# The W1 and W3 blocks of a streamed FFN in transfers of 256 rows instead of 512

## The chip, the cores and the metric

The kernel runs on one core of a Trainium2 chip, in one launch. The metric is the device time of that core in microseconds (us), the median of several executions. The profile comes from one execution, taken by the hardware profiler.

## The reference

The input is `x`, 2048 tokens of 576 features, in bfloat16. Four residual blocks follow each other: a recurrent attention layer, a gated FFN, and the same two once more with the same weights.

```python
x = x + _A_ref(_layernorm(x), mem0, Wq, Wk, Wv, Wo, seg_len=32)   # 64 segments, 8 memory rows carried along
x = x + _B_ref(_layernorm(x), w1, w3, w2)
x = x + _A_ref(_layernorm(x), mem0, Wq, Wk, Wv, Wo, seg_len=32)
x = x + _B_ref(_layernorm(x), w1, w3, w2)

def _B_ref(x, w1, w3, w2):                 # w1, w3: 576 x 4608; w2: 4608 x 576
    gate = jnp.einsum('bsd,df->bsf', x, w1)
    up   = jnp.einsum('bsd,df->bsf', x, w3)
    return jnp.einsum('bsf,fd->bsd', _silu(gate) * up, w2)
```

The attention layer takes 32 tokens at a time; each segment attends to itself and to 8 memory rows that the segment before has produced, so its 64 segments are a chain. It has 32 heads of 128.

## The kernel before

The two attention layers run interleaved: the second follows the first by eight segments, and each of the 72 steps handles one segment of each layer, where both are under way. All attention weights stay in SBUF. The FFN works on groups of 128 tokens (four segments). A job takes a group of the first layer and, where there is one, a group of the second together, 256 columns, and goes through 4608 hidden features in 18 blocks of 256, called pairs. Its weights are too large to stay, so every job streams them from HBM again.

For a pair, `load_w13` fills one of two slots of the tile `W13` (128 partitions x 9 chunks x 256 columns, bfloat16). Chunks 0 to 3 hold rows 0 to 511 of W1, chunks 4 to 7 those of W3, and chunk 8 holds the last 64 rows of both, W1 in partitions 0 to 63 and W3 in partitions 64 to 127. The text calls the first two *blocks* and the last two *tails*. `load_w2` fills one of two slots of `W2C`.

On TensorE the pair is two pieces of work that stand apart in the order. `ffn_up` without `tail` (letter `F` in the order) multiplies the eight chunks of the blocks; `ffn_up` with `tail` (letter `f`) multiplies the tails, in the mode in which TensorE works on two halves of 64 rows. Each run of matmuls begins with the weight load (LDWEIGHTS) that waits for its transfer. Tanh on ScalarE, two products on VectorE and `ffn_down` with W2 follow.

The order of TensorE's work is written out by hand as strings of letters (`FIRST`, `FOUR` eleven times, `LAST`). Everything else is ordered by `plan`, a list scheduler that runs when the kernel is built, with an estimated duration for each piece and with slots as resources; a `W13` load is one piece in it, whatever number of transfers it issues. The order so found is then fixed on every engine. All loads named above are issued by SyncE (SP in the profile), one after the other, from `dma` (line 600). An issue waits until TensorE has read the old content of the place, and the program gives SP's transfers eight semaphores in turn, so that an issue also waits until the transfer eight places before it has landed. The trace shows these as SP's waits for PE and for DMA.

The last job of all finds the attention weights no longer needed and loads its FFN weights into their place in larger transfers (`tail_load`).

Of the kernel before, what the change touches and what calls it, by code (L numbers as in the profile page):

```python
# [13 lines left out]
P = 128  # L14
# [553 lines left out]
class Emitter:  # L568
# [122 lines left out]
    def load_w13(self, pr, w13):  # L691
        def f(n):
            fa = pr * 2 * P
            W = self.T.W13[:, w13.i]
            for kind, wd in ((0, self.a.w1), (1, self.a.w3)):
                self.dma(W[:, 4 * kind:4 * kind + 4], wd[0:4 * P, fa:fa + 2 * P].rearrange("(c p) f -> p c f", p=P))
            for kind, wd in ((0, self.a.w1), (1, self.a.w3)):
                self.dma(W[kind * R64:(kind + 1) * R64, 8], wd[4 * P:D, fa:fa + 2 * P])
        return f
# [628 lines left out]
```

## Time and profile before

| | |
|---|---|
| median of 7 runs | 2695.61 us (2690.09 to 2698.95) |
| the profiled execution | 2695.15 us, span 2693.4 us |
| granted TensorE clock, mean | 0.994 |
| PE (matmul) busy | 2628.0 us, 98% of the span |
| DVE, ACT, POOL busy | 78%, 51%, 12% |
| `W13` loads | 306: 612 blocks of 256 KB, 612 tails of 32 KB |
| `W2C` loads | 306 of 288 KB |
| moved by DMA | 322.08 MB, mean 120 GB/s |

PE is TensorE's matmuls, PEld its weight loads, DVE is VectorE, ACT ScalarE, POOL GpSimd; SPq is SyncE's queue, which issues transfers. A row of a wait says who waited for whom, the sum in us, how often, and the longest. In a timeline the first column is the start in us, the second the time from the first instruction's start to the last one's end, and what stands in brackets is the idle time before and what ended it. Line 591 of the kernel records every matmul, line 594 every operation of ScalarE, line 597 every one of VectorE, and line 600 every transfer that SP issues, so groups are told apart by tiles. The tiles `W13` and `W` both show as `W`; a transfer `W<-in_B_w_dram` fills `W13`, but for 16 of the last job.

### The profile page before, as it was taken

To read this page: it belongs to the slowest core of one execution; us is meant where nothing else is said; L and a number is where in the kernel's file an instruction comes from. 1 tells how busy PE (TensorE), PEld (TensorE's weight loads), DVE (VectorE), ACT (ScalarE), POOL (GpSimd) and SP (SyncE) were. 2 spreads that over 40 slices of the span, in tenths; PEclk is the share of its full clock that TensorE was granted. 3 is DMA by queue.
4 is the path that set the end of the run, shared out by engine and by line. 5 is a ranking of instruction groups with operands and counts; after the bars stand their busy time and mean duration, and the time that the engine had idled before them with its cause. 6 is when DMAs were issued, how large, how long until landed. Compare 5 with 4: busy or idle time off the path is not lost.

```text
span 2693.4 us, 137075 instructions
## 1 busy us (share of the span) xinstructions
PE 2628.0 (98%) x60995; PEld 2285.4 (85%) x60995; DVE 2103.3 (78%) x5463; ACT 1362.8 (51%) x3938; POOL 332.4 (12%) x400
## 2 busy tenths in 40 slices
PE   5999999999999999999999999999999999999998
PEld 4788888888888888888888888888888888888886
DVE  5787886887878788787878878787877878787776
ACT  2655554544545454454545455454545545454542
POOL 1111110110101011010101101010111101011110
PEclk8999999999999999999999999999999999999999
DMA  9064524243442334344233434424243442434457
GB/s 317 5 185 128 149 84 129 78 128 109 117 126 80 111 88 128 108 117 126 80 113 86 128 108 117 127 80 118 83 125 108 117 129 67 118 89 135 128 168 246
DMA packets 478178, 322.08 MB, mean 120 GB/s; under 512 B 26024, under 2 KB 467760, under 8 KB 476944
## 3 DMA queue, kind: packets, MB, share of 16 engines
q1 hardware_dynamic: 474048, 305.43, 38.6%
q8 instruction: 477, 7.82, 1.2%
q0 software_dynamic: 3024, 6.93, 0.9%
q10 hardware_dynamic: 512, 0.94, 0.2%
q14 instruction: 117, 0.96, 0.1%
HBM read 308.49 MB, written 2.36 MB: 115 GB/s over the span
## 4 chain that ended last, share of the span: by engine, by line
PE 86%; DVE 5%; DMA 3%; ACT 3%; issue 1%; SPq 1%; POOL 0%; ACTq 0%; DVEq 0%
PE bank L591 86%; DMA W<-in_B_w_dram 2%; ACT V L594 2%; DVE STAT L597 1%; SPq L600 1%; DVE HTT L597 1%; DVE PB L597 1%; DVE SME L597 1%; DMA W<-in_A_Wk_dram 1%; DVE V L597 1%; DMA WO<-in_A_Wo_dram 0%; DMA XN<-in_A_x_dram 0%; ACT PTS L594 0%; ACT SME L594 0%; DVE PTS L597 0%
## 5 line engine op out<-in xcount | busy, mean ns | idle before, releaser
L591 PEld LDWEIGHTS <-W 128*128 128x128 bf16 (+2 forms) x32176 | 1266.7, 100 | 129.8 <-issue 60.4
L591 PE MATMUL bank<-HT,W 128*128 128x80 bf16 (+3 forms) x23040 | 810.6, 197 | 18.9 <-issue 7.7
L591 PE MATMUL bank<-XTB,W 128*64 128x256 bf16 (+5 forms) x9136 | 660.6, 263 | 6.8 <-DMA W<-in_B_w_dram 3.2
L594 ACT ACTIVATE QKT<-bank 128x64 bf16<-128x64 f32 (+2 forms) x1500 | 349.7, 311 | 351.1 <-PE bank L591 345.1
L1006 POOL MEMSET PB<- 128x1024 bf16 x288 | 274.1, 952 | 1832.4 <-PE bank L591 1539.7
L591 PE MATMUL bank<-OT,WO 128*128 128x80 bf16 (+3 forms) x11520 | 407.5, 198 | 3.4 <-ACT OT L594 1.3
L591 PEld LDWEIGHTS <-WO 128*128 128x128 bf16 (+1 forms) x11520 | 380.4, 102 | 20.8 <-issue 8.9
L594 ACT ACTIVATE V<-bank 64x512 bf16<-64x512 f32 (+1 forms) x606 | 343.1, 585 | 94.7 <-PE bank L591 86.0
L591 PE MATMUL bank<-WV,HT 128*32 128x512 bf16 (+5 forms) x3584 | 373.8, 382 | 1.6 <-DMA WV<-in_A_Wv_dram 1.0
L591 PE MATMUL bank<-W2C,HTT 128*64 128x288 bf16 (+1 forms) x3072 | 322.8, 286 | 1.5 <-issue 1.0
L597 DVE TENSOR_REDUCE STAT<-SME 104x8 f32<-104x320 f32 (+1 forms) x576 | 274.3, 476 | 10.7 <-ACT SME L594 5.3
L597 DVE TENSOR_TENSOR PB<-SME,STAT 40x128 bf16<-40x128 f32 (+4 forms) x912 | 274.9, 336 | 8.5 <-DVE STAT L597 0.5
L594 ACT ACTIVATE HTT<-bank 128x512 bf16<-128x512 f32 (+1 forms) x324 | 176.6, 553 | 206.6 <-PE bank L591 205.0
L597 DVE SCALAR_TENSOR_TENSOR XR<-bank,XR 128x288 f32<-128x288 f32 x576 | 245.9, 446 | 24.2 <-PE bank L591 20.0
L591 PEld LDWEIGHTS <-HT 128*32 128x32 bf16 (+5 forms) x3584 | 154.2, 98 | 125.4 <-issue 17.9
L597 DVE SCALAR_TENSOR_TENSOR HTT<-HTT,bank 128x512 bf16<-128x512 bf16 (+1 forms) x324 | 201.7, 623 | 74.5 <-ACT HTT L594 70.5
L591 PEld LDWEIGHTS <-HTT 128*64 128x64 bf16 (+1 forms) x3136 | 223.5, 105 | 35.3 <-issue 2.5
L594 ACT ACTIVATE OT<-bank 128x320 bf16<-128x320 f32 (+1 forms) x420 | 155.2, 403 | 148.9 <-PE bank L591 146.0
L597 DVE TENSOR_TENSOR HTT<-HTT,bank 128x512 bf16<-128x512 bf16 (+1 forms) x324 | 203.6, 628 | 27.8 <-DVE HTT L597 0.5
L594 ACT ACTIVATE SME<-SME 104x320 f32<-104x320 f32 (+1 forms) x288 | 135.2, 470 | 166.5 <-DVE SME L597 164.7
L597 DVE CAST QKT<-bank 128x128 bf16<-128x128 f32 (+4 forms) x548 | 147.7, 317 | 83.5 <-PE bank L591 81.3
L594 ACT ACTIVATE PTS<-bank 128x320 bf16<-128x320 f32 (+1 forms) x383 | 143.8, 403 | 133.2 <-PE bank L591 120.1
(61 smaller groups left out, 1831.7 us busy)
## 6 DMA issues: line engine op xcount, KB each, us to landing
W<-in_B_w_dram SPq DMA_DIRECT2D x612, 256.0 KB, 3.6
W2C<-in_B_w_dram SPq DMA_DIRECT2D x306, 288.0 KB, 3.3
W<-in_B_w_dram SPq DMA_DIRECT2D x612, 32.0 KB, 3.4
W<-in_B_w_dram SPq DMA_DIRECT2D x8, 1024.0 KB, 12.4
W<-in_A_Wq_dram SPq DMA_DIRECT2D x9, 512.0 KB, 9.2
WO<-in_A_Wo_dram SPq DMA_DIRECT2D x4, 1152.0 KB, 18.1
XR<-in_A_x_dram POOLq DMA_DIRECT2D x16, 288.0 KB, 3.6
WV<-in_B_w_dram SPq DMA_DIRECT2D x4, 1152.0 KB, 10.4
```

The lines of the kernel that those rows point to most:

```text
L591: self.ch("PE", self.nc.tensor.matmul(out, lhsT=lhsT, rhs=rhs, start=start, stop=stop, skip_group_check=True, **k))
L594: self.ch("ACT", self.nc.scalar.activation(*a, **k))
L597: self.ch("DVE", getattr(self.nc.vector, fn_)(*a, **k))
L600: self.ch("SP", self.nc.sync.dma_start(out=out, in_=in_))
L1006: return lambda n: self.ch("POOL", self.nc.gpsimd.memset(self.T.PB[:, pb.i], 0.0))
```

## The change

Each block of 512 rows is loaded in two transfers of 256 rows (two chunks each). The tails stay as they are, and still come after all blocks of the load. A load thus issues six transfers, four of 128 KB and two of 32 KB, instead of four, two of 256 KB and two of 32 KB.

```diff
             W = self.T.W13[:, w13.i]
             for kind, wd in ((0, self.a.w1), (1, self.a.w3)):
-                self.dma(W[:, 4 * kind:4 * kind + 4], wd[0:4 * P, fa:fa + 2 * P].rearrange("(c p) f -> p c f", p=P))
+                for c in (0, 2):
+                    self.dma(W[:, 4 * kind + c:4 * kind + c + 2], wd[c * P:(c + 2) * P, fa:fa + 2 * P].rearrange("(c p) f -> p c f", p=P))
             for kind, wd in ((0, self.a.w1), (1, self.a.w3)):
                 self.dma(W[kind * R64:(kind + 1) * R64, 8], wd[4 * P:D, fa:fa + 2 * P])
```

The order of instructions on PE, DVE, ACT and POOL is the same in both built programs. On SP the 612 blocks become 1224, at the same places. In the built programs SP's transfers rise from 1592 to 2204, and PE's waits on transfers from 1564 to 2178: the first weight load of every half of a block now waits for its own transfer.

## The prediction

> **What bounds the kernel now.** First the page's busy times and the chain that ended last.
>
> ```profile
> PE 2628.0 (98%) x60995; PEld 2285.4 (85%) x60995; DVE 2103.3 (78%) x5463; ACT 1362.8 (51%) x3938; POOL 332.4 (12%) x400
> ...
> PE 86%; DVE 5%; DMA 3%; ACT 3%; issue 1%; SPq 1%; POOL 0%; ACTq 0%; DVEq 0%
> ```
>
> TensorE works 98% of the span, in an order that the change leaves alone. A change to loads can therefore move the time only through TensorE's remaining idle time. The list of waits tells how much of that is owed to the `W13` loads, and what SP itself waits for.
>
> ```profile
> PEld L591 <- issue: 133.7, 431, 4.2
> ...
> PEld L591 <- DMA W<-in_B_w_dram: 8.3, 14, 1.3
> ...
> PE bank L591 <- issue: 9.3, 10, 2.3
> ...
> PE bank L591 <- DMA W<-in_B_w_dram: 3.2, 7, 1.2
> ...
> SPq L600 <- PE bank L591: 1858.0, 754, 74.4
> ...
> SPq L600 <- DMA W<-in_B_w_dram: 2.3, 3, 1.5
> ```
>
> TensorE stood 8.3 + 3.2 = 11.5 us on these transfers; that is all that earlier landings could bring. SP spends 1858 us waiting for TensorE to free a slot, and 2.3 us on earlier `W` transfers: the slots, not the bandwidth, decide when a load starts. What it costs to issue one, and how long one takes to land, is in the rows of line 600, of tile `W`, and of the issues.
>
> ```profile
> L600 SPq DMA_DIRECT2D W<-in_B_w_dram x1240: 367/476/4080, 46.5 to 2672.5; - x178
> ...
> DMA to landing us min/median/max: 2.0/3.5/14.8
> ...
> W<-in_B_w_dram SPq DMA_DIRECT2D x612, 256.0 KB, 3.6
> ...
> W<-in_B_w_dram SPq DMA_DIRECT2D x612, 32.0 KB, 3.4
> ```
>
> An issue takes SP 0.48 us (median). A tail of 32 KB needs 3.4 us, nearly as long as a block eight times its size, though the fastest `W` transfer landed in 2.0 us: the tail stands behind the blocks. Last, one load in the timelines of SP and of PE.
>
> ```profile
> 861.21 2.12 SPq L600 DMA_DIRECT2D W<-in_B_w_dram  x4
> 863.94 0.88 SPq L600 DMA_DIRECT2D W2C<-in_B_w_dram  x2
> 865.50 2.33 SPq L600 DMA_DIRECT2D W<-in_B_w_dram  x4
> ...
> 866.07 0.39 PE L591 MATMUL bank<-XTB,W 64*128 64x256 bf16 x4
> 866.96 0.56 PE L591 MATMUL bank<-XTB,W 64*128 64x256 bf16 x4 [0.50 <-DMA W<-in_B_w_dram]
> ```
>
> Four issues take 2.12 us, so one follows another every 0.55 us. The waiting matmul has 64 rows: it is the tails' piece. The tails are issued last and, in the hand-written order, often wanted first.
>
> How common that is I tallied from the trace: for each transfer of a `W13` load, the landing against the start of the weight load on PE that waits for it, wherever both are recorded (1069 of 1224). Half the blocks land 6.8 us or more ahead of their use, half the tails 7.0. Under 1 us ahead are 10 of 531 blocks and 42 of 538 tails, and 20 tails were waited for. If every transfer landed later by the same d, TensorE would stand longer by the sum, over loads, of what d exceeds the slack: 4.2 us for d = 0.3, 7.9 for 0.5, 12.3 for 0.7, 25.1 for 1.1, 51 for 1.7.
>
> **The change, part by part.** *Two more issues per load.* 612 x 0.55 = 337 us of SP time. It comes out of SP's 1858 us of waiting for TensorE, so in sum it is covered. Without that cover it would be the price itself. Locally the densest stretch I found is 1010.55 to 1029.75: 22 issues in 19.2 us, which need 22 x 0.55 = 12.1. Five loads among them add ten issues, and 17.6 us still fit. So SP does not run behind for good; what remains is lateness inside a load, and of what SP issues right behind it. The `W2C` transfers (264 tallied, 5 under 1 us ahead) add under 1 us by the same sum, and the 15 `XN` loads are not among PE's waits in the steady part, so I put both at nothing.
>
> *Where the tails land.* Only the issue of the last tail is sure to move: from 1.53 us behind the load's first issue to 1.53 + 2 x 0.55 = 2.63. Whether it lands later depends on what it stood behind. The load at 704.91 had a free queue: its last tail landed 2.77 us after its issue, at +4.30. Afterwards it cannot be earlier than 2.63 + 2.0 = +4.63 and would be +5.40 with the old 2.77, so d = 0.33 to 1.1. The load at 861.21 had a full queue: its last tail took 4.34 us and landed at +5.87. The same bytes stand ahead of it afterwards, so if the queue never runs dry it lands when it did, d = 0. The bounds are thus 0 and 1.1. Below nothing is possible only if smaller pieces are served faster (the third rival). At its densest the queue moved 164 packets of 512 bytes in 0.25 us (packet records of the load at 1010.55), 336 GB/s. That is 0.78 us for a block and 0.39 for a half, less than the 0.55 between issues. So SP will no longer fill the queue faster than it drains, and tails will land closer to the 2.0 than to the 3.4. I take d = 0.5, nearer the free queue's low end: 7.9 us.
>
> *Where the blocks land.* The first half of W1 is issued when the block was. Its second half is issued 0.55 later, but is half as long; W3's second half is issued at 1.65 instead of 0.55. Blocks rarely are what TensorE waits for (10 of 531 under 1 us), and the tally has them in.
>
> *614 more waits on PE, 614 more on SP.* Of the runs of 16 weight loads of `F` for 256 columns, 101 with two such waits took 1634 to 1649 ns from first to last matmul, and the one without took 1648. A wait whose transfer has landed costs nothing. SP's added waits are part of the 0.55.
>
> *The eight semaphores in turn.* Eight issues last 8 x 0.55 = 4.4 us, above the 3.5 us median landing, so the wait for the eighth before stays short, as the 2.3 us show. But a load with its `W2C` now takes seven of the eight, so it binds where landings take 5 us. That is one reason why the range reaches past d = 1.1.
>
> *The end.* Behind the last `W13` load (2643.05) SP issues the larger loads of the last job, and TensorE waited 1.17 us for one of them at 2681.19. Two issues more push these by 0 to 1.1 us; I take 0.5.
>
> Sum: 7.9 + 0.5 = 8.4 us on the profiled 2695.15, so 2703.5. The median of the runs is 0.5 us above that execution, so I predict 2704.
>
> A rule speaks against the change. Row first: the blocks land in 3.6 us while issues are 0.55 us apart, so some six transfers are in flight together and share what is fixed in that time. The Trainium skill, "DMA: Bandwidth & Descriptors", section "Bandwidth", says to batch transfers to at least 1 MiB, and its section "Anatomy of one DMA" puts a constant of about 2.0 us on each DMA (measured from GpSimd). Were that paid one after the other, 612 more would add an estimated 1224 us; this trace's overlap speaks for the 8 us.
>
> **The rivals.** *No change: the DMA queue sets the landing anyway.* For it: many of the tight loads look like the one at 861.21, with tails taking over 4 us, so their d may be 0 to 0.3. Against: loads like that at 704.91 are among the tight ones too (0.67 us of slack). Time: 0 to +4 us, 2695 to 2700.
>
> *SP becomes the pace of the load: d of 1.1 or more.* If a transfer takes the same time from issue to landing whatever stands ahead, each tail is 1.1 us later, and the second load of a burst later still. For it: tails in free queues still took 2.8 us. Against: the 2.0 minimum and the free time in the densest stretch. Price: 25.1 us, and up to 37 us if some loads come 1.4 us late; 2709 to 2733.
>
> *Faster: shorter queue.* Halves stand in the queue only briefly, so a tail issued 1.1 us later is served 1.4 us sooner (3.4 down to 2.0) and lands 0.3 us earlier; the twenty waited-for tails get up to 0.3 us each, some 4 us, and at most the whole 11.5, with some of the 9.3 us of "issue" idle if instruction fetches also get through sooner. It decides if half-block transfers cut a tail's landing time by more than the 1.1 us that they delay its issue. Against: the same bytes stand ahead, arriving no earlier. Time: 2684 to 2692.
>
> **How the numbers follow.** The forecast (d about 0.3 to 0.7, +4 to +14 us) gets 0.50, no change 0.24, SP's pace 0.13, faster 0.13. About 0.2%, 5.4 us, is what a measurement here can tell from no change. Of the forecast 0.08 lies below that, so slower is 0.42 + 0.13 = 0.55, same 0.08 + 0.24 = 0.32, faster 0.13. The range 2692 to 2722 takes in the forecast, no change and the 25.1 us of SP's pace, and leaves out nearly all of the faster case and the upper part of SP's pace, under 0.2 together.
>
> **What would show it.** In the profile of the changed kernel: PE's waits on `W` transfers go from 11.5 to about 20 us, at 64-row matmuls; SP's wait for PE falls by some 300 us; six issues of a load take about 3.2 us; tails land in 2.3 to 2.9 us at the median instead of 3.4, halves in about 3. I am wrong if tails still take 3.4 us (then SP's pace is the case), if PE's waits on `W` do not grow, or if the time moves with these waits unchanged.

## The result, and the profile after

The changed kernel takes 2701.33 us (median of 11 runs, 2699.03 to 2706.30), beside 2693.19 for the kernel before (29 runs, 2690.09 to 2699.44): a ratio of 1.0029, 95% interval [1.0021, 1.0036], or +8 us. The profiled span went from 2693.4 to 2702.4 us. The forecast was +8.4 us.

The page after: TensorE is busy 4.2 us longer with the same matmuls (mean granted clock 0.993, before 0.994), and of the chain that ended last transfers hold 4% instead of 3%.

```profile
PE 2632.2 (97%) x60995; PEld 2287.3 (85%) x60995; DVE 2102.5 (78%) x5463; ACT 1362.3 (50%) x3938; POOL 332.4 (12%) x400
...
PE 83%; DVE 8%; DMA 4%; ACT 2%; SPq 1%; issue 1%; POOL 0%; ACTq 0%; DVEq 0%
```

The list of waits (who waited for whom: us in total, times, longest) has most of the loss: TensorE's rows on `W` have grown (before 8.3 and 3.2 us), and its matmuls' row on `W2C` went from 0.4 to 5.0 us. SP's slack has shrunk but is far from gone.

```profile
PEld L591 <- issue: 134.9, 430, 4.1
...
PEld L591 <- DMA W<-in_B_w_dram: 15.1, 28, 1.3
...
DVE LNS L597 <- DMA XN<-in_A_x_dram: 10.6, 10, 1.8
...
PE bank L591 <- DMA W<-in_B_w_dram: 7.8, 12, 1.1
...
PE bank L591 <- issue: 6.4, 6, 2.3
...
PE bank L591 <- DMA W2C<-in_B_w_dram: 5.0, 6, 2.0
```

```profile
SPq L600 <- PE bank L591: 1671.6, 1008, 71.0
...
SPq L600 <- DMA W<-in_B_w_dram: 5.7, 5, 4.5
```

The transfers that TensorE waits for are the tails, as the prediction had it. Of the 6.8 us that the weight loads' row on `W` grew, 5.2 are at weight loads of 64 rows; the lines before and after:

```profile
L591 PEld LDWEIGHTS <-W 64*128 64x128 bf16 x5904 | 143.1, 96 | 55.9 <-issue 26.6 <-DMA W<-in_B_w_dram 6.7
```

```profile
L591 PEld LDWEIGHTS <-W 64*128 64x128 bf16 x5904 | 143.6, 96 | 62.2 <-issue 28.2 <-DMA W<-in_B_w_dram 11.9
```

Issues cost what they did, and both halves and tails land sooner after their own issue (the rows of line 600, of tile `W`, and of the issues with KB and median us to landing).

```profile
L600 SPq DMA_DIRECT2D W<-in_B_w_dram x1852: 367/460/4874, 46.3 to 2682.1; - x186
```

```profile
DMA to landing us min/median/max: 2.0/2.8/15.5
```

```profile
W<-in_B_w_dram SPq DMA_DIRECT2D x1232, 128.0 KB, 2.9
...
W<-in_B_w_dram SPq DMA_DIRECT2D x612, 32.0 KB, 2.6
```

Tails land 2.6 us after their issue instead of 3.4, but are issued so much later that they arrive later all the same. Where two loads follow each other on SP, what stands behind them is late by more. Before, the two loads at 331.71 were issued in 6.78 us, and the `W2C` transfers behind them at 338.59 landed 1.7 us ahead of their use. The timelines of SP and of PE after:

```profile
332.06 8.47 SPq L600 DMA_DIRECT2D W<-in_B_w_dram  x12
340.63 1.05 SPq L600 DMA_DIRECT2D W2C<-in_B_w_dram  x2
```

```profile
345.24 0.42 PE L591 MATMUL bank<-W2C,HTT 128*128 128x288 bf16 x2 [0.56 <-DMA W2C<-in_B_w_dram]
346.02 0.90 PE L591 MATMUL bank<-W2C,HTT 128*128 128x288 bf16 x6 [0.37 <-DMA W2C<-in_B_w_dram]
```

With four more issues ahead of them the same `W2C` transfers are issued at 340.63; the trace has the first landing at 345.19, and the matmul starts at 345.23. Of the 2.0 us by which their issue is later, 0.8 is what the whole program is late by then. The first of them also took longer to land, 4.56 us instead of 3.38, for a reason that the trace does not name.

All seven of the matmuls' and weight loads' waits for `W2C` (5.0 and 0.7 us) stand in three places, near 150, 345 and 2574 us, each time behind two or three loads in a row; there is none in between. The last of the three, behind 18 issues:

```profile
2557.73 11.72 SPq L600 DMA_DIRECT2D W<-in_B_w_dram  x18
2569.55 2.16 SPq L600 DMA_DIRECT2D W2C<-in_B_w_dram  x2
```

By the start of the same weight loads, the changed kernel falls behind by 3.6 us between 140 and 160 us of the kernel before, by 1.3 between 340 and 360, and by 3.4 between 2560 and 2580; in the whole of the profile it is 9.0.

### The profile page after: what moved, and what is told of

It is laid out like the page before. It is cut to its first block, busy times and chain, and to the rows that moved or that the text cites. A ratio compares the mean times of both kernels' runs of the same rounds, so it can differ in the third digit from the quotient of the medians.

```text
span 2702.4 us, 138301 instructions
## 1 busy us (share of the span) xinstructions
PE 2632.2 (97%) x60995; PEld 2287.3 (85%) x60995; DVE 2102.5 (78%) x5463; ACT 1362.3 (50%) x3938; POOL 332.4 (12%) x400
## 4 chain that ended last, share of the span: by engine, by line
PE 83%; DVE 8%; DMA 4%; ACT 2%; SPq 1%; issue 1%; POOL 0%; ACTq 0%; DVEq 0%
PE bank L591 83%; DMA W<-in_B_w_dram 2%; DVE STAT L597 2%; SPq L600 1%; DVE HTT L597 1%; DVE SME L597 1%; DVE PB L597 1%; ACT V L594 1%; DMA XN<-in_A_x_dram 1%; DMA W<-in_A_Wk_dram 1%; DVE V L597 1%; DVE LNS L597 1%; DVE XN L597 1%; DMA WO<-in_A_Wo_dram 0%; DMA W2C<-in_B_w_dram 0%
## 5 line engine op out<-in xcount | busy, mean ns | idle before, releaser
L597 DVE SCALAR_TENSOR_TENSOR XR<-bank,XR 128x288 f32<-128x288 f32 x576 | 245.8, 446 | 25.1 <-PE bank L591 20.9
```

The costliest lines, as they stand in the source:

```text
L597: self.ch("DVE", getattr(self.nc.vector, fn_)(*a, **k))
```

## The experiments

Each ran beside the kernel before on one chip, and its ratio is to those runs; three chips were used, on which the kernel before took 2693.39 to 2694.97 us, so kernels of different chips are compared by their ratios. The theory: SP issues one transfer every 0.55 us, and what stands behind more issues lands later. The rivals: halves cost in themselves (their size in the DMA queue, or TensorE's 614 more waits), or only the bytes count.

TensorE runs the same instructions in the same order in all of them, so I also compare, by the start of the same weight loads, how the span grew in three stretches: up to 365 us of the kernel before, 365 to 2520 (the steady part), and the rest, in which the last job runs. These come from one profile each. A profiled execution lies up to 5 us from its kernel's median, so the medians decide on the time and the stretches tell where it lies. By the traces' clock records TensorE ran at half its clock for 28 to 43 us of each profile but the quarters' (before 32, after 38), nearly all of it in the first and the last stretch; growth of a few us there is not owed to loads alone.

| kernel | ratio, 95% interval | median us | to 365 | steady | end |
|---|---|---|---|---|---|
| the change | 1.0029 [1.0021, 1.0036] | 2701.33 | +2.1 | +3.5 | +3.4 |
| W1 alone in halves | 0.9994 [0.9985, 1.0002] | 2692.80 | -3.6 | +0.3 | +4.2 |
| quarters | 1.0986 [1.0972, 1.1001] | 2960.54 | +50.5 | +192.0 | +23.5 |
| whole blocks, tails in two | 1.0024 [1.0015, 1.0033] | 2700.81 | +0.8 | +3.2 | +2.7 |
| tails first, always | 1.0033 [1.0020, 1.0045] | 2703.90 | +0.6 | +3.1 | +0.2 |
| tails first where used first | 0.9974 [0.9964, 0.9984] | 2687.16 | -2.1 | -3.0 | -1.2 |
| halves, tails by GpSimd | 0.9972 [0.9961, 0.9983] | 2686.69 | -4.4 | -4.4 | -2.0 |
| whole blocks, tails by GpSimd | 1.0000 [0.9991, 1.0008] | 2692.97 | +3.4 | -4.0 | +2.3 |
| before, `W2C` merged | 1.0016 [1.0007, 1.0025] | 2698.34 | +3.5 | -1.3 | +0.2 |
| the change, `W2C` merged | 1.0039 [1.0025, 1.0054] | 2703.30 | +2.2 | +2.7 | +2.6 |
| the change, tails first where used first | 1.0014 [1.0006, 1.0023] | 2696.58 | -0.9 | 0.0 | -0.6 |

**W1 alone in halves.**

```diff
-                for c in (0, 2):
-                    self.dma(W[:, 4 * kind + c:4 * kind + c + 2], wd[c * P:(c + 2) * P, ...])
+                st = 2 if kind == 0 else 4
+                for c in range(0, 4, st):
+                    self.dma(W[:, 4 * kind + c:4 * kind + c + st], wd[c * P:(c + st) * P, ...])
```

> Only the blocks of W1 come in halves, those of W3 stay whole: 306 more issues instead of 612, and the last tail is issued 0.55 us later than before instead of 1.1. Theory (the pace of SP's issues makes the tails and what follows them late): the tally of slacks gives 2 to 4 us for a lateness of 0.2 to 0.3 us, so 2695 to 2698, about half of the whole change. Rival (the time moved for another reason, such as the 614 more waits on TensorE): half as well if it goes with the waits, 0 if it was chance between two builds.

Measured was no change; a rise of over 0.5 us is outside the interval. The last tail landed 0.30 us later (median, from the load's first issue: 5.63 us instead of 5.33), as expected, but PE's waits on `W` hardly moved, and the steady part grew by 0.3 us. The theory's 2 to 4 us did not come: the loss does not go in proportion to the issues, and the tally had promised too much for a small lateness.

**Quarters.** Both blocks in four transfers of 128 rows.

```diff
-                for c in (0, 2):
-                    self.dma(W[:, 4 * kind + c:4 * kind + c + 2], wd[c * P:(c + 2) * P, ...])
+                for c in (0, 1, 2, 3):
+                    self.dma(W[:, 4 * kind + c:4 * kind + c + 1], wd[c * P:(c + 1) * P, ...])
```

> Every block in four transfers of 128 rows: six more issues per load than before, the last tail is issued 1.53 + 6 x 0.55 = 4.83 us behind the first block and lands at 6.8 to 7.1, where it landed at 4.3 to 5.9: 1.0 to 2.8 us later. Theory (SP's pace): the tally of slacks gives 25 us for 1.1 and 81 for 2.2, so +25 to +80 us, 2720 to 2775, and PE's waits on W and W2C transfers grow by about that. Rival (the DMA queue sets the landing, the same bytes land when they did): at most twice the change's, 2700 to 2710.

It cost 266 us, over three times the upper end. TensorE's busy time, its waits, and SP's timeline in a dense part:

```profile
PE 2724.6 (92%) x60931; PEld 2337.4 (79%) x60995; DVE 2108.5 (71%) x5463; ACT 1363.4 (46%) x3938; POOL 332.8 (11%) x400
```

```profile
PEld L591 <- DMA W<-in_B_w_dram: 176.6, 154, 5.0
...
PE bank L591 <- DMA W<-in_B_w_dram: 136.9, 127, 4.7
```

```profile
1012.18 25.76 SPq L600 DMA_DIRECT2D W<-in_B_w_dram  x40
```

Forty issues, four loads, take 25.76 us: the median from one to the next is 0.48 us, and SP stands still once for long, 2.9 us at 1023.1. Four loads need most of that time on SP, so that lateness can add up from load to load, which a tally of one lateness per load cannot show (2.3 us for the last tail, 7.60 against 5.33; that alone would be some 80 us). The queue is not the limit: tails here land 2.1 us after their issue. That only the bytes count falls with this run.

Not all of the 266 us is waiting for transfers. By the matmul rows `W` grew by 134 us and `W2C` by 17. The same matmuls were also busy 97 us longer, at a mean granted clock of 0.968 instead of 0.994: the clock records have 42 stretches at half clock, 191 us together, where the kernel before has 6 of 32 us. Of this trace's 34 pauses of TensorE over 2 us, 31 have such a stretch beginning in the pause or within 4 us of its end. So more than a third of the loss is slower matmuls, which go with the pauses; no run here separates them from the waits.

**Whole blocks, tails in two transfers of 32 rows.** As many issues as in the change, no block cut.

```diff
             for kind, wd in ((0, self.a.w1), (1, self.a.w3)):
-                self.dma(W[kind * R64:(kind + 1) * R64, 8], wd[4 * P:D, fa:fa + 2 * P])
+                for h in (0, 32):
+                    self.dma(W[kind * R64 + h:kind * R64 + h + 32, 8], wd[4 * P + h:4 * P + h + 32, fa:fa + 2 * P])
```

> Blocks whole as before; each tail in two transfers of 32 rows instead of one of 64. As many issues as in the changed kernel (six per load, the last at +2.63 us), but no block is cut. Theory (what counts is how many issues stand ahead of the last tail): as the changed kernel or a little more, +6 to +12 us, 2699 to 2705. Rival (what costs is that blocks come in halves: their size, their own waits on TensorE): no change, 2691 to 2695.

As the theory had it: 1.0024, the change's own loss within the intervals, without a single half. The last tail lands at 5.82 us from the first issue; in the change it is 5.84. TensorE's weight loads wait for `W` as there:

```profile
PEld L591 <- DMA W<-in_B_w_dram: 12.3, 26, 2.0
```

In the built program TensorE has as many waits on transfers as in the change, 2178, so this run does not exclude those as the cause; the one with tails by GpSimd does.

**Tails first.** The kernel before with its two loops exchanged.

```diff
-            for kind, wd in ((0, self.a.w1), (1, self.a.w3)):
-                self.dma(W[:, 4 * kind:4 * kind + 4], wd[0:4 * P, ...])
             for kind, wd in ((0, self.a.w1), (1, self.a.w3)):
                 self.dma(W[kind * R64:(kind + 1) * R64, 8], wd[4 * P:D, fa:fa + 2 * P])
+            for kind, wd in ((0, self.a.w1), (1, self.a.w3)):
+                self.dma(W[:, 4 * kind:4 * kind + 4], wd[0:4 * P, ...])
```

> The four transfers of before, but both tails are issued ahead of both blocks. Theory (tails are late because they are issued last): PE's waits at 64-row matmuls, most of 11.5 us, go away; blocks are issued 1.1 us later and by the tally cost 4 us of waits; and in 189 of 306 loads the old tails are released later than the old blocks, mostly by 0.3 to 0.7 us, which now holds the blocks up too. Together -6 to +5 us, 2687 to 2698, with waits moved from 64-row to 128-row matmuls. Rival (only the number of issues and bytes counts): no change in time and in the kind of waits.

The last tail landed at 3.29 us from the load's first issue instead of 5.33 (median), and the 64-row matmuls of full width no longer wait for it, but the time rose by 0.33%, some 9 us, beyond the +5 that I had allowed. The groups of `F`'s 128-row weight loads and of `f`'s matmuls, with their idle time before and what ended it, and VectorE's wait for the input rows:

```profile
L591 PEld LDWEIGHTS <-W 128*128 128x128 bf16 x20960 | 850.7, 99 | 74.3 <-issue 26.6 <-DMA W<-in_B_w_dram 9.4 <-DMA W<-in_A_Wk_dram 4.2
...
L591 PE MATMUL bank<-XTB,W 64*128 64x256 bf16 x1008 | 84.3, 271 | 0.9 <-DVE V L597 0.9
```

```profile
DVE LNS L597 <- DMA XN<-in_A_x_dram: 18.1, 13, 1.9
```

The wait has moved from the tails to the blocks (9.4 us; before 1.3), and most loads use their blocks first. That is a wait taken away from one transfer and given to the next in the queue. How much of it comes from the tails' places being released later than the blocks', which I had also expected, this run does not tell.

**Tails first only where used first.** The planner knows, when the loads are written out, which of the two pieces of a pair it has placed first; 116 of 306 loads get their tails first.

```diff
                 last_up[:] = [fm, ff]
+                if not last:
+                    w13.use = (fm, ff)
...
+            tails_first = w13.use[1].start < w13.use[0].start
+            for what in ((1, 0) if tails_first else (0, 1)):      # 1: the loop over the tails, 0: over the blocks
```

> The four transfers of before; the tails are issued ahead of the blocks only in the loads whose tails TensorE's order uses first (114 of 304 tallied in the trace of before), else behind them. Theory (lateness of the tails, by their place in SP's issue order, is what TensorE waits for): most of PE's 11.5 us on W at 64-row matmuls goes, without the waits of tails-first in all loads: -9 to -3 us, 2684 to 2691. Rival (as in the run with all tails first, the wait moves to the blocks and to what SP issues behind): 0 to +8 us, with waits at 128-row matmuls.

It beats the kernel before, 2687.16 us, and by what was expected. TensorE's waits, and the groups of `f`'s weight loads and matmuls (the edit moves lines down by two: 593 is the matmuls' line here, 599 VectorE's):

```profile
PEld L593 <- DMA W<-in_B_w_dram: 5.2, 9, 1.5
...
PE bank L593 <- DMA W<-in_B_w_dram: 3.2, 5, 1.3
```

```profile
L593 PEld LDWEIGHTS <-W 64*128 64x128 bf16 x5904 | 142.8, 96 | 51.0 <-issue 28.1 <-DMA W<-in_B_w_dram 1.4
...
L593 PE MATMUL bank<-XTB,W 64*128 64x256 bf16 x1008 | 84.3, 271 | 0.9 <-DVE V L599 0.9
```

The same transfers in the same number, only their order on SP differs; the 64-row matmuls of full width do not wait for `W` any more, and the 64-row weight loads wait 1.4 us instead of 6.7. The blocks pay little for it: their 128-row weight loads of full width wait 2.4 us instead of 1.3. The matmuls' row in total is the 3.2 us of before, but 2.6 of them now lie behind 2520 us. These rows show 3 us less waiting; by the ratio the time fell by 7, and the rest is not in them.

**Halves, with the tails issued by GpSimd.** SP issues four transfers per load, as before the change.

```diff
-                self.dma(W[kind * R64:(kind + 1) * R64, 8], wd[4 * P:D, fa:fa + 2 * P])
+                self.swdma(W[kind * R64:(kind + 1) * R64, 8], wd[4 * P:D, fa:fa + 2 * P])
```

> The changed kernel's halves, but the 612 tails are issued by GpSimd instead of SP: SP issues four transfers per load, as before the change, and no tail stands behind four halves on SP. Theory (SP's issues set the lateness): PE's waits on W and W2C fall from 22.9 and 5.0 us to 12 or less, and the time to that of before or below, 2686 to 2696, unless GpSimd's own queue, where a tail now waits for its slot ahead of the PB memsets, holds up the softmax; that would show as waits of VectorE for POOL and can cost 10 us and more. Rival (blocks in halves cost in themselves): 2699 to 2704 with PE's waits on W as in the changed kernel.

**Whole blocks, tails issued by GpSimd.** The same edit in the kernel before.

> The kernel before, blocks whole, with the 612 tails issued by GpSimd: SP issues two blocks per load instead of four halves. It asks whether halves cost anything once tails do not stand behind them. Theory (what costs is the tails' and the later loads' place behind SP's issues): as the run with halves and tails on GpSimd or a little faster, -10 to -5 us against before, 2685 to 2690. Rival (a half costs in itself, through the DMA queue or the waits on TensorE): clearly faster than that run, by 4 us or more, below 2683.

Halves without the tails behind them on SP: 0.9972, some 15 us below the change. TensorE's waits, and GpSimd's:

```profile
PEld L591 <- DMA W<-in_B_w_dram: 3.4, 6, 1.4
...
PE bank L591 <- DMA W<-in_B_w_dram: 2.1, 3, 1.3
...
POOL W L606 <- PE bank L591: 815.6, 174, 11.7
```

No wait for `W2C` is left in the list. The run moves the tails to another queue as well as to another issuing engine, and does not separate the two. GpSimd now waits 815.6 us for slots ahead of its PB memsets, and TensorE's waits for it stay at 0.3 us. So halves, with some 610 more waits on TensorE than before, cost nothing in themselves; that rival falls. The run with whole blocks I had placed at 2685 to 2690, and it came at 2692.97: clearly *slower* than the one with halves (ratios 1.0000 and 0.9972), the side that I had not listed. With whole blocks, 612 issues fewer on SP thus saved no time. In the steady part the two agree (-4.4 and -4.0), and TensorE waits there for `W` 0.4 us in the one and not at all in the other; the profiles put the whole difference into the first 365 us and the last job. A good half of it is "issue", idle time in which TensorE waited for nothing that the profile shows:

```profile
PE bank L591 <- issue: 13.7, 16, 3.4
```

In the run with halves that row is 6.6. The other part goes with the clock: TensorE's matmuls are busy 2628.9 us with whole blocks and 2623.0 with halves, at a granted clock of 0.992 and 0.994. The profiles differ by 12.4 us, the medians by 6.3, so some of this is one execution's chance. Over the runs whose trace has every matmul, the "issue" row is 3.1 to 7.9 us where both blocks come in halves, and 7.2 to 13.7 where both are whole. In the traces of tails in two and of tails first, 64 matmul records are missing, which leaves gaps of 0.16 us that count as "issue"; without those of the steady part they have 8.7 and 4.3 us, and the second breaks the pattern. That blocks in halves let TensorE's instructions through sooner is not shown by any run: this stays open.

**`W2C` merged.** The two `W2C` loads of neighbouring pairs as one transfer, in the kernel before and in the change.

```diff
+            if pr % 2 == 0 and w2.mate.i in (None, 1) and w2.i == 0:
+                return                       # the second of the two loads both slots
...
+            self.dma(self.T.W2C[:, w2.i - lo + 1:w2.i + 1].rearrange("p s b d -> p (s b) d"), ...)
```

> Before, with the two W2C loads of two neighbouring pairs as one transfer of 576 KB instead of two of 288 KB: 153 issues fewer, blocks and tails untouched. Theory (issues ahead in SP's queue make the loads behind late): W13 loads behind a W2C load are issued 0.55 us earlier; PE's waits on W fall by 1 to 4 us: -4 to 0 us, 2689 to 2694. Rival (the pace of bytes counts): 0; and as the merged transfer can only start when both slots are free, W2C waits could rise instead, 0 to +4 us.

> The changed kernel with the W2C loads merged in the same way: 2051 issues on SP instead of 2204. Theory (SP's issues): part of the change's loss comes back, -1 to -5 us against the changed kernel, 2696 to 2700. Rival (blocks in halves cost in themselves): as the changed kernel, 2701.

Both are misses. With 153 issues fewer the profile is 1.3 us shorter in the steady part and longer elsewhere (1.0016 in all); on the change nothing came back (1.0039). As the rival of the first had it, waits for `W2C` rose, from 0 to 2.5 us ahead of weight loads and from 0.4 to 2.2 ahead of matmuls. A transfer of 576 KB lands in 4.1 us instead of 3.3, and can start only when both slots are free. Fewer issues are no gain if the transfer that is wanted becomes later. That this is the whole loss is not shown: "issue" idle of the matmuls rose as well, from 9.3 to 12.2 us.

**The change, with tails first where used first.** The edit of the run with that order, with the loop over the blocks in halves.

> The changed kernel with the tails ahead of the blocks in the loads whose tails are used first. Theory: the tails' part of the loss goes (PE's waits on W from 22.9 to about 10 us), what stands behind two loads on SP, W2C above all (5.0 us), stays late: 2688 to 2696, 5 to 13 us below the changed kernel, and 0 to 6 us above the same order with whole blocks (2687). Rival (halves cost in themselves): it stays 6 to 9 us above that, 2693 to 2697.

By the time alone the rival fits better: 2696.58 lies just above what the theory gave (2688 to 2696) and within what the rival gave (2693 to 2697). It is 9 us by the medians, 11 by the ratios, above the same order with whole blocks, where the theory had 0 to 6 and the rival 6 to 9. TensorE's waits on `W` fell from 22.9 to 15.4 us by the sum of both rows, not to some 10. The matmuls' rows, with weight loads on `W` at 10.2:

```profile
PE bank L593 <- DMA W<-in_B_w_dram: 5.2, 10, 1.4
...
PE bank L593 <- DMA W2C<-in_B_w_dram: 5.0, 8, 1.2
```

The same order with whole blocks has 3.2 and 0.4. So part of the tails' loss is repaired, and the `W2C` part is not, as the theory had said. These rows explain 7 us by the matmuls (2.0 and 4.6), while "issue" idle is 4.1 us lower; the two profiles differ by only 4.6 us. That halves cost nothing in themselves rests on the run with tails by GpSimd; what the rest of the difference is stays open.

## Why the prediction was right, and where its terms were off

*Two more issues per load, 337 us of SP.* Measured: the durations of SP's issues sum to 865.9 us before and 1203.4 after, 337.5 more. SP's wait for TensorE fell by only 186 us where I had said some 300; where the other 150 came from the list does not name.

*Tails later by d = 0.5.* The last tail is issued 2.92 us behind the load's first issue instead of 1.73 (medians), 1.2 us later, and its landing went from 5.33 to 5.84 us. Halves land in 2.9 us and tails in 2.6, within what was forecast. That bounds from a free and a full queue enclose the truth held; that tails would be served sooner, but not by as much as they are issued later, held too.

*TensorE's waits on `W`, +7.9 us.* The rows rose by 6.8 (weight loads) and 4.6 (matmuls). My 11.5 us of waiting before was a mistake in reading: a stall stands in both rows, as the one at 866.96 does, with 0.78 us for the weight load and 0.50 for the matmul, and I had added them. The term was 1 to 3 us too large. The mechanism was right: the matmuls' growth is all at those of 64 rows.

*`W2C` at nothing.* This step failed. I had given these transfers a price under 1 us; behind two loads in a row they were issued 2 us later, and TensorE's matmuls waited 5.0 us for them instead of 0.4. The densest stretch that I used to show that SP keeps up lies in the steady part, where no wait for `W2C` arose; all stand in the first 365 us and behind 2520, where two or three loads follow each other: SP keeps up on average, not there. `XN`, also put at nothing, had VectorE wait 10.6 us instead of 2.0; it is in no wait of TensorE.

*The end, 0.5 us.* Behind the last `W13` load, from 2643 us on, the span grew by 0.2 us, and the wait at 2681.19 went from 1.17 to 1.05, so the term was small as forecast. The 3.4 us that the table has behind 2520 lie between 2560 and 2580, at the three loads in a row shown above; they belong to `W2C` (1.5 us) and a tail (1.08).

*What balanced it.* TensorE's "issue" idle of the matmuls fell from 9.3 to 6.4 us, above all by a pause of 2.0 us at 212.6 that is gone; the third rival had named such a gain, but its cause is not shown. By the matmul rows: +4.6 for `W`, +4.6 for `W2C`, -2.9 for issue, 6.3 of the 9.0 us of span; the matmuls' busy time grew by 4.2 us, and smaller rows take 1.5 off. So the sum came within a microsecond partly by luck, because errors of opposite sign met: `W` was a little too large, `W2C` too small.

*Waits on PE at nothing.* The run with halves and tails by GpSimd has the extra waits and is, with the one ordered by use, the fastest of all; they cost nothing that shows.

*The rivals.* That the DMA queue sets the landing anyway is refuted by tails that land 0.5 us later here and 2.3 with quarters; that SP's pace takes over was wrong at two halves and right at four quarters; faster was wrong for this edit, though halves were faster than whole blocks, for a reason left open, once the tails did not stand behind them. The second rival's 2709 does not follow from its own price of 25.1 us and more, which gives 2720 as the lower end.

*The rule.* Every transfer here takes some time to land, however small (2.1 us for tails behind quarters, 2.9 for a half; the shortest of a tail in two parts took 1.6). But these times overlap and are not the price: 612 transfers more cost 8 us.

## What to carry to other kernels

Cost a split of transfers by the issuing queue, not by the bytes: so many issues times the pace, and then ask which transfers stand *last* behind them and how early they are used; look behind two or three loads in a row, not at the average. Before splitting or merging, put the transfers into the order in which their data is used: here that alone brought 0.26% (2687.16 us), and issuing the tails from an engine that was 12% busy brought 0.28% with the blocks in halves (2686.69 us) and nothing with whole blocks (2692.97). Lateness is nearly free while it fits into the slack, and then costs far more than in proportion: +0, +8 and +266 us for one, two and six more issues per load, the last with 97 us of slower matmuls in it.

## What was not expected of the hardware

The pace of SP is not the same for all small transfers: with tails in two of 32 rows the issues of all `W` transfers took 0.48 us on average, against 0.56 before and 0.54 in the change. The same transfers as before, with the tails first, took 0.59. And two kernels that differ only in halves or whole blocks, both with at most 0.4 us of waits for `W` in the steady part, agree there to 0.4 us over 2155 us, yet differ by 12 us in their profiles at the two ends, where the clock differs too.
